# Chunk work moved between the steps of the first block, one fused attention and two-layer kernel

## The chip, the cores and the metric

The kernel runs on one core of one Trainium2 chip. The metric is device microseconds of one execution of the whole program, from launch to end, the median over runs. The core has a matrix engine (PE, with PEld for its weight loads), a vector engine (DVE), a scalar engine (ACT), a general engine (POOL), and a sync engine (SP) whose queue issues all DMAs here. Each engine takes its own instructions in the order in which they were written.

## The reference

```
for t in range(S):                                    # B=4, H=8, S=768, D=48
    state = alpha[:, :, t, :, None] * state + einsum('bhd,bhe->bhde', k[:, :, t], v[:, :, t])
    y[:, :, t] = einsum('bhd,bhde->bhe', q[:, :, t], state)
x = y.transpose(0, 2, 1, 3).reshape(B * S, H * D)     # 3072 tokens x 384
h = x @ w_in ;  x = (max(h, 0) + m_alpha * min(h, 0)) @ w_out          # 384 -> 2048 -> 384
h = x @ w_in2;  out = where(h >= 1, h, where(h <= -1, 0, (h + 1)**2 / 4)) @ w_out2
```

A linear attention with a decay per channel and token feeds two dense layers. The four weight matrices arrive as 64-bit floats and are turned into 32-bit floats on the chip.

## The kernel before

**Attention.** The tokens are cut into 24 chunks of 128, six in each batch element. For a chunk c the kernel transposes the decays (`fetch(c, 2)`, line 210 on PE, then `clamp` on DVE, line 202), the keys (`fetch(c, 1)`) and the queries (`fetch(c, 0)`). Two scans over the decays follow on DVE: `at_scan(c, "R")` (line 257) and `at_scan(c, "F")` (lines 263 and 264). `K2` is the keys times R, `Q2` the queries times F (line 274). `at_kt` transposes K2 back (`kt`, line 280 on PE) and ACT copies it to SBUF (`KT`, line 282). `at_gain` (line 337), `at_states` and `at_decay` carry the state from chunk to chunk, `at_within` makes the scores inside a chunk (lines 305 and 319, then `A`, line 324), and `at_out` (lines 372 and 305) the outputs, which ACT and DVE split into a high and a low word in `xs` (lines 394 to 401); six small DMAs (line 408) bring the shared rows to their place. The transposes of decays, keys, queries and K2 of the chunks 4 to 9 all use one PSUM tile, tag `at`, with a single buffer: each must be read out before the next is written. The chunks 10 and later are transposed on DVE instead.

**Layers.** A step is one block of 512 tokens by one of 16 slices (`fc`) of the hidden dimension. `do_h(s)` makes nine matmuls `hp` (line 512), ACT then scales them (`g`, line 526), DVE takes the maximum (line 530), ACT rounds it to `gh` (line 531), DVE makes the remainder `gl` (line 533). `do_out(s - 1)` follows on PE with nine matmuls from the step before (line 553). The products keep a high and a low word of both operands, hence nine. Block 0 is the tokens of the chunks 0 to 3, so those four run first, in the opening, a loop over `c` of its own; the steps s = 0 to 15 are block 0.

**Weights.** In block 0 each step also prepares later weights. `w1_load(fc + 5)` issues seven DMAs into one of three buffers; `w1_words` makes two ACT passes over the 32-bit words of the 64-bit floats (part 0 is line 440, part 1 line 442), in place; `w1_join(fc + 2)` puts them together in two DVE passes (lines 448 and 451), which frees the buffer; `w1_split` makes the high word on ACT (`wh`, line 490) and the low one on POOL (`wl`, line 496), which the matmuls two steps later need.

**What sets the order.** The kernel writes the order out by hand. Four tables say what chunk work goes where: `pres[s]` ahead of step s, `acts[s]` inside `emit_act` between `gh` and `gl`, `mids[s]` after `do_h(s)` and its weights, `ends[s]` after `do_out(s - 1)`. A chunk c of 4 to 7 starts at step s = 2 + 3(c - 4) and takes n = 3 steps, later ones n = 4. Where `acts` has an entry, both join passes of the step stand ahead of `hp`'s maximum; otherwise one does, and the other stands between `gh` and `gl`. `fetch(c, 0)` also issues the loads of chunk c + 2 on SP, behind the six small DMAs of `at_out`.

Of the kernel before, what the change touches and what calls it, by code (L numbers as in the profile page):

```python
# [22 lines left out]
def kernel(  # L23
# [593 lines left out]
    def put(where, s, *fs):  # L617
        where.setdefault(s, []).extend(fs)
# [4 lines left out]

    put(mids, 0, lambda: fetch(NC0, 2))
    put(ends, 0, lambda: at_scan(NC0, "R"), lambda: fetch(NC0, 1), lambda: at_mul(NC0, "K2", nc.vector))
    put(mids, 1, lambda: at_scan(NC0, "F"))
    put(ends, 1, lambda: at_kt(NC0), lambda: at_decay(NC0))
    put(acts, 2, lambda: fetch(NC0 + 1, 2))
    for c in range(NC0, NCH + 1):
# [11 lines left out]
        if c + 1 < NCH:  # L641

            put(pres if s + 1 < NFC else ends, s + 1, lambda c=c: at_scan(c + 1, "R"))
            if c + 1 < NPE:
                put(ends, s + (n - 2 if direct(c + 1, 1) else 1), lambda c=c: fetch(c + 1, 1))
            put(ends, s + n - 2, lambda c=c: at_mul(c + 1, "K2", nc.vector))
            put(ends, s + n - 1, lambda c=c: at_kt(c + 1), lambda c=c: at_decay(c + 1))
            put(pres if s + n - 1 < NFC else ends, s + n - 1, lambda c=c: at_scan(c + 1, "F"))
        if c + 2 < NPE:
            put(acts, s + 2, lambda c=c: fetch(c + 2, 2))  # L650
        if c == NPE - 2:
# [9 lines left out]
    with tc.manual_schedule():  # L661
# [8 lines left out]
        def w1_words(i, part=None):  # L670
            if 0 <= i < NFC:
                conv_words(0, i, part)
# [119 lines left out]
        for c in range(NC0):  # L792
# [6 lines left out]
            if c < NC0 - 1:  # L799
                at_kt(c + 1)  # L800
            if c + 2 < NC0:
                at_scan(c + 2, "R")
                at_scan(c + 2, "F")
# [15 lines left out]
            if i >= 0:  # L819
                w1_split(i)  # L820
        load_chunk(NC0 + 1, nc.sync)
        mps = ps_h.tile([P, NFC], F32, tag="h", name="mps", padded_shape=[P, 512])
        nc.tensor.transpose(out=mps, in_=ma, identity=ident[0:NFC, 0:NFC])
# [3 lines left out]
        for s in range(len(steps) + SK):  # L827
            if s < len(steps):
                j, fc = steps[s]
                if j == 0:  # L830
                    full = s in acts
                    run_slots(pres, s)
                    w1_join(fc + 2, None if full else 0)
                do_h(s, (lambda: w1_words(fc + 3, 0),
                         lambda: run_slots(acts, s) if full else w1_join(fc + 2, 1)) if j == 0 else None)
# [7 lines left out]
            if s < NFC:  # L843
                w1_words(fc + 3, 1)
            if s < len(steps):
# [197 lines left out]
```

## Time and profile before

| | us |
|---|---|
| median of 3 runs (lowest to highest) | 945.85 (945.71 to 948.45) |
| the profiled execution, its own time | 945.43 |
| its span, first to last instruction | 943.6 |
| PE busy | 905.5 |
| DVE busy | 482.2 |
| ACT busy | 406.7 |
| POOL busy | 361.4 |

The time of the profiled execution lies 1.8 us above its span: that is launch and end. In the rows below block 0 is cut where the `hp` of a step starts: step 0 at 40.94 us, step 2 at 55.49, step 5 at 75.97, step 8 at 97.51, step 11 at 120.38, step 14 at 139.84. PE is busy for nearly all of the span; its idle time stands almost wholly in the first 155 us, which are the opening and block 0. The mean granted TensorE clock is 0.987 of 2.4 GHz; the stretches at half of it stand in the same 155 us.

### The profile page before, as it was taken

The page shows a single profiled execution, that of the slowest core. Times are in us where ns is not written, and L with a number is a line of the kernel's source. Part 1 is how long each engine was busy: PE and PEld are TensorE (multiplying, and loading weights), DVE is VectorE, ACT ScalarE, POOL GpSimd, SP SyncE. Part 2 cuts the span into 40 slices and gives each one's busy share as a digit, 9 for nine tenths or more (in the row PEclk, how much of TensorE's full clock was granted, in tenths as well). Part 3 has the DMA queues.
Part 4 walks back from the last instruction along what each step waited for, and adds up shares of the span by engine and source line. Part 5 has one row for each costly group of instructions (what it writes and reads, how often), then busy time and mean ns, then how long its engine had stood idle before and what let it go on. Part 6 is the DMA issues. An engine that isn't in the chain of part 4 may idle for free.

```text
span 943.6 us, 17329 instructions
## 1 busy us (share of the span) xinstructions
PE 905.5 (96%) x6955; PEld 770.2 (82%) x6955; DVE 482.2 (51%) x692; ACT 406.7 (43%) x654; POOL 361.4 (38%) x294
## 2 busy tenths in 40 slices
PE   7787899999999999999999999999999999999996
PEld 5676677788888788788788899999999999999995
DVE  7598764766765666665322234435334334344333
ACT  2555554443444434444355533345554333333332
POOL 4233222643544344443267732332332332333231
PEclk9899999999999999999999999999999999999999
DMA  9785735554654545442143210212220200200001
GB/s 165 173 164 125 167 87 160 137 141 124 190 140 124 145 113 155 130 128 65 42 161 107 76 60 1 77 47 62 84 67 1 67 1 1 68 1 1 34 1 38
DMA packets 119897, 85.58 MB, mean 91 GB/s; under 512 B 64752, under 2 KB 105472, under 8 KB 119808
## 3 DMA queue, kind: packets, MB, share of 16 engines
q1 hardware_dynamic: 119808, 84.39, 34.5%
q8 instruction: 56, 0.92, 0.4%
q14 instruction: 33, 0.27, 0.1%
HBM read 66.66 MB, written 15.73 MB: 87 GB/s over the span
## 4 chain that ended last, share of the span: by engine, by line
PE 87%; DVE 4%; DMA 3%; SPq 2%; issue 2%; ACT 2%; DVEq 0%; ACTq 0%
PE hp L512 40%; PE y_oo L553 12%; PE y_yy L564 7%; PE y_oo L564 7%; PE y_o L553 6%; PE y_o L564 3%; PE y_at L564 3%; DMA nat<-in_alpha_dram 2%; PE w L372 1%; SPq L408 1%; PE w L305 1%; PE kt L280 1%; PE w L337 1%; PE tr L210 1%; PE w L319 1%
## 5 line engine op out<-in xcount | busy, mean ns | idle before, releaser
L544 POOL TENSOR_TENSOR gl<-g,gh 128x512 fp32r<-128x512 f32 x175 | 233.4, 1333 | 454.3 <-ACT gh L543 444.2
L512 PE MATMUL hp<-xs,wh 128*128 128x512 f32 x1152 | 367.8, 401 | 3.8 <-issue 3.2
L512 PEld LDWEIGHTS hp<-xs,wh 128*128 128x128 f32 x1152 | 212.1, 190 | 44.0 <-issue 4.9
L512 PE MATMUL hp<-xs,wl 128*128 128x512 f32 x576 | 227.9, 396 | 0.0
L543 ACT CAST gh<-g 128x512 fp32r<-128x512 f32 x177 | 109.4, 618 | 211.5 <-DVE g L542 143.9
L540 DVE SCALAR_TENSOR_TENSOR g<-g 128x512 f32<-128x512 f32 (+1 forms) x97 | 67.7, 697 | 207.7 <-ACT g L524 206.3
L512 PEld LDWEIGHTS hp<-xs,wl 128*128 128x128 f32 x576 | 109.3, 190 | 24.1
L526 ACT ACTIVATE g<-hp,malpha 128x512 f32<-128x512 f32 x96 | 66.2, 689 | 139.2 <-PE hp L512 139.1
L538 DVE TENSOR_TENSOR g<-hp,g 128x512 f32<-128x512 f32 x80 | 55.2, 690 | 102.7 <-ACT g L526 102.2
L524 ACT ACTIVATE g<-hp,half 128x512 f32<-128x512 f32 (+1 forms) x97 | 66.5, 686 | 94.0 <-PE hp L512 94.0
L542 DVE TENSOR_TENSOR g<-hp,g 128x512 f32<-128x512 f32 (+1 forms) x97 | 66.5, 686 | 3.4
L496 POOL TENSOR_TENSOR wl<-wf,wh 128x768 fp32r<-128x768 f32 x16 | 30.5, 1904 | 79.5 <-ACT wh L490 59.5
L553 PE MATMUL y_oo<-gh,wh 128*128 128x512 f32 x192 | 60.5, 397 | 0.0
L553 PE MATMUL y_oo<-gl,wh 128*128 128x512 f32 x192 | 60.1, 394 | 0.4 <-POOL gl L544 0.4
L553 PE MATMUL y_oo<-gh,wl 128*128 128x512 f32 x192 | 60.0, 394 | 0.0
L243 DVE STREAM_TRANSPOSE T<-nat 128x512 f32<-128x512 f32 x42 | 43.4, 1086 | 0.0
L553 PEld LDWEIGHTS y_oo<-gl,wh 128*128 128x128 f32 x192 | 36.3, 189 | 8.6 <-POOL gl L544 0.8
L553 PEld LDWEIGHTS y_oo<-gh,wl 128*128 128x128 f32 x192 | 36.4, 189 | 7.9
L553 PEld LDWEIGHTS y_oo<-gh,wh 128*128 128x128 f32 x192 | 36.1, 190 | 7.4
L399 DVE TENSOR_TENSOR xs<-w,xs 128x384 fp32r<-128x384 f32 x24 | 13.4, 557 | 50.4 <-ACT x L398 45.5
L210 PE MATMUL tr<-ident,nat 128*128 128x128 f32 x120 | 23.0, 328 | 16.7 <-DMA nat<-in_alpha_dram 11.4
L553 PE MATMUL y_o<-gl,wh 128*128 128x512 f32 x96 | 38.1, 396 | 0.0
(127 smaller groups left out, 1397.2 us busy)
## 6 DMA issues: line engine op xcount, KB each, us to landing
wst<-in_moe_w_out_dram SPq DMA_DIRECT2D x32, 384.0 KB, 4.6
wst<-in_moe_w_in_dram SPq DMA_DIRECT2D x16, 384.0 KB, 4.2
w_d<-wf SPq DMA_DIRECT2D x16, 384.0 KB, 2.7
w<-w_d SPq DMA_DIRECT2D x16, 384.0 KB, 3.1
x_d<-ev SPq DMA_DIRECT2D x18, 256.0 KB, 2.3
x2s<-x_d SPq DMA_DIRECT2D x18, 256.0 KB, 3.6
out_dram<-ev SPq DMA_DIRECT2D x24, 192.0 KB, 2.0
al<-in_alpha_dram SPq DMA_DIRECT2D x12, 384.0 KB, 3.3
```

Of the source, the lines that this page charges most:

```text
L210: nc.tensor.transpose(out=ps[:, p, :], in_=nat_of(c, i)[:, 2 * p:2 * p + 2, :].rearrange("t h d -> t (h d)"), identity=ident)
L243: nc.vector.transpose(out=tin(c, i).rearrange("f n (j g) -> f n g j", g=4), in_=natq[:, n].rearrange("j n (g f) -> j n g f", g=4)[:, :, :, ...
L512: nc.tensor.matmul(out=hp, lhsT=w[:, p, :], rhs=xs[:, x, p, :], start=(i == 0), stop=(i == 3 * ND - 1))
L524: nc.scalar.activation(y, x, AF.Relu, bias=half, scale=0.5)
L526: nc.scalar.activation(y, x, AF.Copy, scale=malpha[:, fc:fc + 1])
L538: nc.vector.tensor_max(out=y, in0=x, in1=y)
L540: nc.vector.scalar_tensor_tensor(out=y, in0=y, scalar=1.0, in1=y, op0=ALU.min, op1=ALU.mult)
L542: nc.vector.tensor_max(out=y, in0=x, in1=y)
L543: nc.scalar.copy(out=hi, in_=y)
L544: (nc.gpsimd if parts == 1 else nc.vector).tensor_sub(out=lo, in0=y, in1=hi.bitcast(F32))
L553: nc.tensor.matmul(out=ops[d], lhsT=w[:, d * P:(d + 1) * P], rhs=g, start=first, stop=last)
L564: nc.tensor.matmul(out=ops[t], lhsT=g[:, t * P:(t + 1) * P], rhs=w, start=first, stop=last)
```

## The change

Four things are written in another place. No arithmetic, tile or DMA is added or dropped.

- The decays of a chunk (`fetch(c, 2)`, with the clamp) are transposed in `acts` of the first step of chunk c - 1; before, they were in the last step of chunk c - 2. `acts` thus has entries at the steps 2, 5, 8, 11 and 14 and not at 2, 4, 7, 10 and 13.
- `at_kt`, the transpose of K2, goes from `ends` to `mids` of the same step (while that step is below 16), that is ahead of `do_out`.
- The two word passes are half a step earlier: part 0 of the weights `fc + 4` at the end of a step, part 1 of `fc + 3` inside `emit_act`. Before, it was part 0 of `fc + 3` inside and part 1 of `fc + 3` at the end.
- The decays, R, keys, K2 and F of chunk 4 are made in the opening, in and behind its last pass, and its `at_kt` in step 0; before, they stood in the steps 0 and 1.

```diff
-    put(mids, 0, lambda: fetch(NC0, 2))
-    put(ends, 0, lambda: at_scan(NC0, "R"), lambda: fetch(NC0, 1), lambda: at_mul(NC0, "K2", nc.vector))
-    put(mids, 1, lambda: at_scan(NC0, "F"))
-    put(ends, 1, lambda: at_kt(NC0), lambda: at_decay(NC0))
-    put(acts, 2, lambda: fetch(NC0 + 1, 2))
+    put(mids, 0, lambda: at_kt(NC0))
+    put(ends, 0, lambda: at_decay(NC0))
...
-            put(ends, s + n - 1, lambda c=c: at_kt(c + 1), lambda c=c: at_decay(c + 1))
+            put(mids if s + n - 1 < NFC else ends, s + n - 1, lambda c=c: at_kt(c + 1))
+            put(ends, s + n - 1, lambda c=c: at_decay(c + 1))
...
-        if c + 2 < NPE:
-            put(acts, s + 2, lambda c=c: fetch(c + 2, 2))
+        if c + 1 < NPE:
+            put(acts, s, lambda c=c: fetch(c + 1, 2))
...
             if c < NC0 - 1:
                 at_kt(c + 1)
+            else:
+                fetch(NC0, 2)
+                at_scan(NC0, "R")
...
         load_chunk(NC0 + 1, nc.sync)
+        fetch(NC0, 1)
+        at_mul(NC0, "K2", nc.vector)
+        at_scan(NC0, "F")
...
-                do_h(s, (lambda: w1_words(fc + 3, 0),
+                do_h(s, (lambda: w1_words(fc + 3, 1 if s else None),
...
-                w1_words(fc + 3, 1)
+                w1_words(fc + 4, 0)
```

The first place is DVE, from the end of the opening to the first `gl`. `T` is the clamped decay of chunk 4, `R`, `K` and `F` are its scans and keys, `wf` the joined weights, `A` the scores of chunk 3. Before:

```order
L324 TENSOR_TENSOR A<-w,mask 128x512
L448 SCALAR_TENSOR_TENSOR wf<-wst 128x768
L399 TENSOR_TENSOR xs<-w,xs 128x3x128
L451 SCALAR_TENSOR_TENSOR wf<-wst,wf 128x768
L448 SCALAR_TENSOR_TENSOR wf<-wst 128x768
L530 TENSOR_TENSOR hp<-hp,g 128x512
L451 SCALAR_TENSOR_TENSOR wf<-wst,wf 128x768
L533 TENSOR_TENSOR gl<-hp,gh 128x512
L202 TENSOR_SCALAR T_104<-tr 128x4x128
L257 SCALAR_TENSOR_TENSOR R<-T_104,zrev 128x516
L274 TENSOR_TENSOR K_738<-tr,R 128x512
```

Now:

```order
L324 TENSOR_TENSOR A<-w,mask 128x512
L202 TENSOR_SCALAR T_104<-tr 128x4x128
L257 SCALAR_TENSOR_TENSOR R<-T_104,zrev 128x516
L448 SCALAR_TENSOR_TENSOR wf<-wst 128x768
L399 TENSOR_TENSOR xs<-w,xs 128x3x128
L451 SCALAR_TENSOR_TENSOR wf<-wst,wf 128x768
L274 TENSOR_TENSOR K_702<-tr,R 128x512
L263 RECIPROCAL zfw<-R 128x4
L264 SCALAR_TENSOR_TENSOR F<-T_104,zfw 128x516
L448 SCALAR_TENSOR_TENSOR wf<-wst 128x768
L530 TENSOR_TENSOR hp<-hp,g 128x512
```

The clamp and R now stand ahead of the last xs of the opening, K2 and F ahead of the first maximum.

The second place is ACT in the steps 4 and 5, with one chunk's `KT` copy. Before:

```order
L526 ACTIVATE g<-hp,malpha 128x512
L440 ACTIVATE wst<-wst 128x768
L531 CAST gh<-hp 128x512
L490 CAST wh_991<-wf 128x768
L282 COPY KT<-kt 128x512
L442 ACTIVATE wst<-wst,mhalf 128x768
```

Now:

```order
L440 ACTIVATE wst<-wst 128x768
L526 ACTIVATE g<-hp,malpha 128x512
L442 ACTIVATE wst<-wst,mhalf 128x768
L531 CAST gh<-hp 128x512
L490 CAST wh_986<-wf 128x768
L282 COPY KT<-kt 128x512
```

The word pass L440 now stands ahead of the activation of `hp`, and L442 between that and `gh`; the `KT` copy still stands behind `gh` and `wh`.

The third place is PE from the end of `hp` of step 4 to the beginning of step 5. Before:

```order
L512 MATMUL hp<-xs,wl_834 128x512
L210 MATMUL tr<-ident,nat 128x128 x4
L553 MATMUL y_oo<-gh,wh_770 128x512 x2
...
L553 MATMUL y_o_778<-gl,wh_770 128x512
L280 MATMUL kt<-ident,K_950 128x128 x4
L512 MATMUL hp<-xs,wh_906 128x512 x2
```

Now:

```order
L512 MATMUL hp<-xs,wl_835 128x512
L280 MATMUL kt<-ident,K_951 128x128 x4
L553 MATMUL y_oo<-gh,wh_782 128x512 x2
...
L512 MATMUL hp<-xs,wl_909 128x512
L210 MATMUL tr<-ident,nat 128x128 x4
L553 MATMUL y_oo<-gh,wh_833 128x512 x2
```

`kt` takes the place of the decays' transpose behind `hp`, and the decays' transpose stands a step later, behind the next `hp`.

## Rows read from the trace of the kernel before

**Rows 1.** The page's busy time of each engine, share of the span, instructions.

```profile
PE 905.5 (96%) x6955; PEld 770.2 (82%) x6955; DVE 482.2 (51%) x692; ACT 406.7 (43%) x654; POOL 361.4 (38%) x294
```

**Rows 2.** Stretches: us, busy PE, PEld, DVE, ACT, POOL (instructions), clock, DMA share, GB/s.

```profile
40.94:55.49 14.55, 11.51 (x40) 9.00 (x40) 10.87 (x13) 8.26 (x12) 3.64 (x2) 0.73 0.87 190
55.49:75.97 20.48, 16.69 (x158) 13.22 (x156) 19.86 (x26) 12.28 (x17) 7.49 (x4) 1.00 0.68 150
75.97:97.51 21.54, 18.42 (x185) 14.68 (x184) 16.46 (x23) 12.82 (x19) 7.27 (x5) 0.92 0.58 127
97.51:120.38 22.87, 19.72 (x194) 15.85 (x193) 16.26 (x23) 12.43 (x18) 7.28 (x5) 0.86 0.74 173
120.38:139.84 19.46, 17.20 (x192) 13.54 (x191) 16.09 (x23) 11.66 (x17) 3.68 (x2) 0.99 0.37 75
```

**Rows 3.** Timeline of PE: start, length, line, tiles, idle before and releaser.

```profile
48.94 1.12 PE L210 MATMUL tr<-ident,nat 128*128 128x128 f32 x4 [3.04 <-DVE T L202]
62.41 0.66 PE L210 MATMUL tr<-ident,nat 128*128 128x128 f32 x4 [1.49 <-DVE T L202]
75.55 0.66 PE L280 MATMUL kt<-ident,K 128*128 128x128 f32 x4 [2.31 <-DVE T L202]
94.61 0.63 PE L210 MATMUL tr<-ident,nat 128*128 128x128 f32 x4 [3.12 <-DMA nat<-in_alpha_dram]
114.60 1.09 PE L210 MATMUL tr<-ident,nat 128*128 128x128 f32 x4 [3.15 <-DMA nat<-in_alpha_dram]
```

**Rows 4.** The chain that ended last: start, length, what.

```profile
50.05 3.19 PE hp L512 x9
76.21 3.66 PE hp L512 x9
97.75 2.08 PE hp L512 x9
```

**Rows 5.** Timeline of DVE and PE at the end of the opening.

```profile
36.62 0.69 PE L372 MATMUL w<-A,v 64*64 64x64 f32 x32 [1.77 <-DVE A L324]
40.92 0.56 DVE L399 TENSOR_TENSOR xs<-w,xs 128x384 fp32r<-128x384 f32 x1 [3.49 <-ACT xs L394]
45.11 0.79 PE L210 MATMUL tr<-ident,nat 128*128 128x128 f32 x4
46.13 0.70 DVE L530 TENSOR_TENSOR hp<-hp,g 128x512 f32<-128x512 f32 x1 [2.54 <-ACT g L526]
```

**Rows 6.** Timeline of DVE: the two scans, at their longest and shortest.

```profile
48.92 2.68 DVE L257 TENSOR_TENSOR_SCAN R<-T,zrev 128x516 f32<-128x516 f32 x1
85.49 1.22 DVE L257 TENSOR_TENSOR_SCAN R<-T,zrev 128x516 f32<-128x516 f32 x1
70.43 2.03 DVE L264 TENSOR_TENSOR_SCAN F<-T,zfw 128x516 f32<-128x516 f32 x1
```

**Rows 7.** Timeline of DVE, ACT and PE in step 4.

```profile
69.63 0.68 DVE L274 TENSOR_TENSOR K<-tr,R 128x512 f32<-128x512 f32 x1
70.57 0.60 PE L210 MATMUL tr<-ident,nat 128*128 128x128 f32 x4
74.21 0.69 DVE L530 TENSOR_TENSOR hp<-hp,g 128x512 f32<-128x512 f32 x1
75.42 0.84 ACT L490 CAST wh<-wf 128x768 fp32r<-128x768 f32 x1
76.25 0.59 ACT L282 COPY KT<-kt 128x512 f32<-128x512 f32 x1
```

**Rows 8.** Timeline of SP's queue and ACT around a chunk's outputs.

```profile
87.11 3.94 SPq L408 DMA_DIRECT2D xs<-x  x6
91.10 0.58 SPq L177 DMA_DIRECT2D nat<-in_alpha_dram  x1
99.93 0.69 ACT L526 ACTIVATE g<-hp,malpha 128x512 f32<-128x512 f32 x1 [0.67 <-PE hp L512]
101.09 0.93 ACT L440 ACTIVATE wst<-wst 128x768 f32<-128x768 f32 x1 [0.47 <-DMA wst<-in_moe_w_out_dram]
```

## The prediction, made before the changed kernel ran

> **What bounds the kernel now.** I read the page first: PE is busy for 905.5 us of a span of 943.6 [rows 1], so only PE's 38 us of idle time, and matmuls that run at half clock, can be won. Next the busy time in stretches, to see where the idle time stands: between the `hp` of step 0 and that of step 14 there are 98.9 us, of which PE is busy 83.5 [rows 2]; the reader is to take busy from length in each row: 3.04, 3.79, 3.12, 3.15 and 2.26 us idle. The timeline of PE then names what ended each of the long waits [rows 3]: two of them DMA of a chunk's decays (3.12 and 3.15), the others the clamp L202, which frees the one PSUM buffer that the next transpose needs (3.04, 1.49, 2.31). Last the chain, for the price of the clock: nine `hp` matmuls take 2.08 us at 2.4 GHz, but 3.19 and 3.66 behind two of the gaps [rows 4], where a stretch at 1.2 GHz follows. DVE is the next bound: it is busy 16.1 to 16.5 us of the 19.5 to 22.9 of three steps [rows 2].
>
> **The sum, stretch by stretch.** All terms are changes against the profiled execution, 945.43 us.
>
> *Opening, up to hp of step 0: +1.0.* The clamp (0.68) and R go ahead of the last xs of the opening; R takes 1.22 to 2.68 [rows 6], long where POOL's wl runs beside it, as it does here. DVE waited 3.49 us just there [rows 5], so both fit. K2 (0.68), the reciprocal (0.17) and F (1.23 to 2.08) meet an idle time of 2.54 ahead of the first maximum [rows 5]: they fit or overrun by 0.4. PE gets two transposes of 0.79 to 1.12 us at half clock [rows 3, 5]; the first stands where PE waited 1.77 for A [rows 5] and costs nothing unless its decays land late, the second is in front of `hp`. Bounds 0 and +1.9, the two together; I take +1.0, the second at its longer price.
>
> *Steps 0 and 1: -5.3.* The wait of 3.04 goes, with the two transposes 0.79 and 1.12 [rows 3, 5]: -4.9. Without that gap the hp of step 1 runs at full clock: 3.19 - 2.08 = -1.1 [rows 4]. Back come 0.7: in step 0 both word passes stand ahead of gh on ACT, and the second, a pass of about 0.9 [rows 8], pushes gh, for which PE then waits. If the clock falls all the same, this term is -4.2.
>
> *Steps 2 to 4: -2.2.* The wait of 2.31 was the clamp of a transpose in step 4, which is now in step 5: it goes, and so does that transpose's own 0.4 on PE's path (of the 0.60 that it is busy [rows 7], as its end overlaps what follows). The 1.49 of step 2 stays: order and work are the same there. I add 0.5 for a new wait: `kt` moves ahead of `do_out`, so K2 must be ready some 2.1 us earlier. In step 4 K2 ended at 69.63 + 0.68 = 70.31, and `hp` at 70.57 [rows 7], so 0.26 is left; as PE closes up by more, some of it is lost. Bounds 0 and 1.0.
>
> *Steps 5 to 7: -3.3.* The decays now have a step more to land: they were issued at 91.10 [rows 8] and awaited until 94.61 [rows 3], 3.5 us, and are used a full step (some 6 us) later: -3.1. The half clock behind the 2.31 goes: 3.66 - 2.08 = -1.6 [rows 4]. New is a wait on the KT copy. The transpose of the decays writes the PSUM buffer that `kt` filled the step before, and ACT empties it only behind gh and wh, and wh waits for DVE's second join. With the rows of step 4: K2 starts at 69.63, then F, a join, the maximum and a join end at 74.21 + 0.69 = 74.9 whatever their order [rows 7]; wh begins there, and the copy ends 0.83 + 0.59 behind the start of wh (75.42 to 76.84) [rows 7], so at 76.3. PE, from hp's end at 70.57, has kt (0.4 to 0.6, as that transpose), `do_out` and hp (nine matmuls each, 2.08 to 2.2 [rows 4]) and comes to 75.1 to 75.6, I take 75.4. So +0.9; bounds 0 (F 0.8 shorter, as the scans can be [rows 6]) and 1.3. With 0.5 for K2 as above: -3.1 - 1.6 + 0.9 + 0.5.
>
> *Steps 8 to 10: -4.1.* The wait of 3.15 goes. Behind it, from 114.60 to the hp at 120.38 PE took 5.78 us at half clock; the same work behind the earlier gap, 94.61 to 97.51, took 2.90 [rows 2, 3]: -2.9. Again +0.9 and +0.5. And +0.5 for the word pass L440, which now stands ahead of the activation L526. Its weights are issued behind six small DMAs and three loads of a chunk. Before, they landed at 101.09, 25.1 us after the hp of step 5 began at 75.97. Half clock (-1.6) is in that. So is SP's queue, which a weight load held until the small DMAs began at 87.11; that load's join is now written ahead of the maximum, which frees the queue sooner by 0 to 4.8 us (no row tells; I take the middle, 2.4). With 0.9 for KT it is 22.0. The hp of step 8 ends 18.1 + 2.1 = 20.2 us after that of step 5 began (18.1: 21.5 less the 3.3 above). So L526 is late by 1.8 and the pass, 2.7. The clamp behind it has about that slack or more, as `do_out` (2.1), the chunk's outputs (0.69 for L372 alone [rows 5]) and its gain stand on PE ahead of the transpose that needs it; but DVE, 16.3 of 18.1 us busy, has 1.8 to spare, and loses some 0.9. I take half of it; bounds 0 and 3.
>
> ACT did wait for such a weight, 0.47 us at 101.09 [rows 8], and nothing on PE followed. The Trainium skill (TensorE: Matmul & The Clock Gate, Architectural detail) says that ScalarE and VectorE take their queues strictly first in, first out, which speaks against the move: whatever stands ahead of L526 holds it. By that rule the full 2.7 or more would go through in each chunk; by the row the cost was nil, since the pass stood behind the activation. It is rival 2 below.
>
> *Steps 11 to 13: -0.4.* Of 2.26 idle all goes [rows 2]; back come 0.9, 0.5 and 0.5 as before. *Steps 14 and 15: +1.3.* The last decays' transpose (0.4) moves in here, with its wait for KT (0.9).
>
> 1.0 - 5.3 - 2.2 - 3.3 - 4.1 - 0.4 + 1.3 = -13.0. Past step 15 PE is bound by its own matmuls, and nothing is moved, so the gain is kept. On the profiled execution: 932.4; on the median of 945.85, which is 0.4 higher: 932.9.
>
> **Rivals.**
>
> 1. *All hides (928).* KT and K2 cost nothing, as F runs at 1.23 rather than 2.03: 4 x 0.9 and 3 x 0.5 less, about -18. For it: the scans do run at 1.22 where POOL is idle [rows 6]. Against: wl runs once a step.
>
> 2. *ACT's queue holds the activations (939).* The word pass waits 2.7 or more behind the chunk's DMAs, and DVE, with no slack, hands it on to PE: +3 in each of two chunks. For it: the rows above and the order. Against: half of the chunks' weights are loaded with the queue free, and the last steps have no loads.
>
> 3. *DVE becomes the pace (937).* Busy 16.3 of three steps, with waits between its ops it needs 20 us for three, not 18.1. The three stretches then give -1.5, -2.9 and +0.5 instead of -7.8: 1.0 - 5.3 - 2.2 - 3.9 + 1.3 = -9.1.
>
> 4. *The load chain makes it slower (951).* If the weights come so late that L526 waits 4.8 us in each of the four chunks' first steps (2.7, and 2.1 more if the queue comes free no sooner) and PE gets all of it: 4 x 4.8 = 19.2 against 14.0 of gain without the two word-pass terms: +5.2. It decides from 14.0 / 4 = 3.5 us a chunk. Against it: the loads are not written later than before, and in just these steps PE has the chunk's outputs to do as well.
>
> 5. *No change (945.6).* From step 2 on the DMA gaps turn into DVE gaps of the same size, and the half clock stays: 1.0 - 5.3 for the opening and the steps 0 and 1, three waits for KT (2.7) and the +1.3 of the end: -0.3. For it: DVE is busy 19.86 of 20.48 in the steps 2 to 4 [rows 2]. Against: 16.3 of 21.5 and less behind them.
>
> **How the numbers follow.** The forecast of 932.9 has a chance of 0.52, its own range is 929 to 937 (KT 0 to 1.3 four times, K2 0 to 1.0 three times, the opening 0 to 1.9, seldom all at one end). Rival 1 has 0.13, rival 2 0.13, rival 3 0.12, rival 4 0.05, rival 5 0.05. Half clock that stays in one place would add 1.1 to 2.9. Eight times in ten I expect 926.5 to 941.5: it takes in the rivals 1 to 3, and leaves out 4 and 5. What a measurement of this kernel can tell from no change is about 0.3%, 943.0 to 948.7: rivals 1 to 3 and the forecast lie below it, so faster has 0.89 (0.90 less 0.01 that may reach into it); same 0.06, slower 0.05.
>
> **What would show it.** In the changed profile, PE's waits on DMA of `nat` are gone or under 1 us; a wait of a decays' transpose on ACT's KT copy of about 0.9 us stands in the steps 5, 8, 11 and 14; no transpose waits over 1 us ahead of step 2; the granted clock is 1.0 from step 1 on; three steps take 18 to 19 us; L526 starts late behind L440 in the steps 8 and 11, and PE does not follow. It is wrong if PE waits longer than 1.5 us for gh, gl or Q in these steps, if the clock falls again, or if the hp of step 14, which by the sum starts at 139.84 - 14.3 = 125.5, starts behind 130.

## The result and the profile after

The changed kernel took 936.63 us (median of 8), the kernel before, taken beside it, 947.9 (median of 8): a ratio of 0.9897, with a 95% interval of 0.9869 to 0.9925. Faster was right, and the time lies in the range, with 0.4 us to spare; the gain is smaller than forecast. The profiled executions say by how much: 945.43 before, 936.41 after, a gain of 9.0 where the sum had 13.0. One execution of each kernel (5042 us of the changed one, 1009 of the one before) is left out of the ratio.

The page of the changed kernel, its first row (busy time, share of the span, instructions), answers to [rows 1]:

```profile
PE 903.9 (97%) x6955; PEld 767.8 (82%) x6955; DVE 487.9 (52%) x692; ACT 405.4 (43%) x654; POOL 362.9 (39%) x294
```

PE's busy time fell by 1.6 us, the span by 9.0, but the 1.6 is the sum of two opposite terms. From the first `hp` of step 0 to that of step 16, PE's idle time fell by 5.9 (16.05 to 10.18) and its busy time by 5.5 (95.57 to 90.07), of which 1.9 are the two transposes that went to the opening and the rest is mostly half clock. In the opening the busy time rose by 3.6 (30.23 to 33.80), as the transposes came in and PE is at half clock up to 45.7 us. (Of the 38 us that PE was idle before, 26.8 stand ahead of step 16, not nearly all.) The stretches of the changed kernel, cut at the same steps as [rows 2] (steps 0–1, 2–4, 5–7, 8–10, 11–13, 14–15; us, busy PE, PEld, DVE, ACT, POOL, clock, DMA share, GB/s):

```profile
43.54:52.38 8.84, 8.32 (x32) 6.18 (x32) 8.27 (x10) 6.95 (x11) 3.46 (x2) 0.88 0.70 144
52.38:71.80 19.42, 16.30 (x151) 12.82 (x150) 17.52 (x21) 12.82 (x18) 7.50 (x5) 1.00 0.84 184
71.80:89.63 17.83, 16.94 (x183) 13.44 (x182) 17.11 (x23) 12.31 (x18) 7.05 (x4) 1.00 0.55 143
89.63:111.76 22.13, 18.52 (x192) 14.68 (x190) 18.72 (x26) 12.39 (x19) 5.86 (x3) 0.92 0.85 174
111.76:129.25 17.49, 17.12 (x191) 13.44 (x190) 16.52 (x22) 10.51 (x16) 7.05 (x4) 1.00 0.57 125
129.25:143.79 14.54, 12.86 (x181) 10.08 (x180) 9.40 (x16) 5.59 (x10) 2.31 (x2) 1.00 0.13 24
```

The reader takes each length from that of [rows 2], with one correction. The cuts there at 120.38 and 139.84 lie inside an `hp`; its first matmul, which is the cut everywhere else, starts at 120.03 and 139.60 (timeline of PE, before):

```profile
120.03 0.96 PE L512 MATMUL hp<-xs,wh 128*128 128x512 f32 x2
...
139.60 0.70 PE L512 MATMUL hp<-xs,wh 128*128 128x512 f32 x2
```

So steps 8 to 10 took 22.52 before, steps 11 to 13 took 19.57, and steps 14 and 15 took 152.56 − 139.60 = 12.96:

| stretch | forecast | measured |
|---|---|---|
| opening, to the first hp (40.94 to 43.54) | +1.0 | +2.6 |
| steps 0–1 | −5.3 | −5.7 |
| steps 2–4 | −2.2 | −1.1 |
| steps 5–7 | −3.3 | −3.7 |
| steps 8–10 | −4.1 | −0.4 |
| steps 11–13 | −0.4 | −2.1 |
| steps 14–15 | +1.3 | +1.6 |
| behind step 15 | 0 | −0.2 |

One row is far off: steps 8 to 10 were to give 4.1 and gave 0.4. The timeline of PE in the changed kernel has the waits that answer to [rows 3] (steps 2, 5, 8, 8, 11–13, 14):

```profile
61.14 0.66 PE L210 MATMUL tr<-ident,nat 128*128 128x128 f32 x4 [2.52 <-DVE T L202]
...
74.92 0.66 PE L210 MATMUL tr<-ident,nat 128*128 128x128 f32 x4 [0.89 <-ACT KT L282]
...
92.93 0.66 PE L210 MATMUL tr<-ident,nat 128*128 128x128 f32 x4 [1.07 <-ACT KT L282]
...
99.51 0.66 PE L210 MATMUL tr<-ident,nat 128*128 128x128 f32 x4 [2.54 <-DVE T L202]
99.93 0.84 PE L512 MATMUL hp<-xs,wh 128*128 128x512 f32 x2
...
103.55 0.74 PE L553 MATMUL y_oo<-gh,wh 128*128 128x512 f32 x2
...
126.68 0.66 PE L280 MATMUL kt<-ident,K 128*128 128x128 f32 x4 [0.32 <-DVE K L274]
...
132.48 0.66 PE L210 MATMUL tr<-ident,nat 128*128 128x128 f32 x4 [1.00 <-ACT KT L282]
```

The waits for DMA of `nat` are gone, all of them. The waits for the KT copy are there at the forecast size (0.89, 1.07, 1.00). And a clamp, L202, holds PE for 2.54 us in step 8, where the sum had 0.5. The hp behind it takes 103.55 − 99.93 = 3.62 us in place of 2.08: a stretch at 1.2 GHz, as this row of the busy time by stretches of the changed kernel has it:

```profile
100.40:103.80 3.40, 3.40 (x10) 2.65 (x9) 2.97 (x6) 1.30 (x3) 1.80 (x1) 0.50 0.90 203
```

What makes the clamp late is seen on ACT and DVE (timeline of the changed kernel, steps 2 and 8; the row of PE is the last matmul of step 8's `hp`, which L526 needs):

```profile
58.28 0.91 ACT L440 ACTIVATE wst<-wst 128x768 f32<-128x768 f32 x1 [2.57 <-DMA wst<-in_moe_w_in_dram]
59.09 0.67 ACT L526 ACTIVATE g<-hp,malpha 128x512 f32<-128x512 f32 x1
...
91.46 0.40 PE L512 MATMUL hp<-xs,wl 128*128 128x512 f32 x1
...
96.68 0.88 ACT L440 ACTIVATE wst<-wst 128x768 f32<-128x768 f32 x1 [3.80 <-DMA wst<-in_moe_w_in_dram]
97.46 0.68 ACT L526 ACTIVATE g<-hp,malpha 128x512 f32<-128x512 f32 x1
98.17 0.70 DVE L530 TENSOR_TENSOR hp<-hp,g 128x512 f32<-128x512 f32 x1 [2.66 <-ACT g L526]
98.78 0.68 DVE L202 TENSOR_SCALAR T<-tr 128x512 f32<-128x512 f32 x1
```

The word pass L440 waits for its weights, the activation L526 stands behind it, the maximum L530 waits for that, and the clamp is written behind the maximum. In step 8 `hp` ends at 91.86 and L526 starts at 97.46, 5.6 us later. This is the mechanism of rival 2, in steps 2 and 8 rather than 8 and 11. The weights of step 8 are issued late by SP's queue (timeline of SP, same kernel):

```profile
82.52 3.95 SPq L408 DMA_DIRECT2D xs<-x  x6
86.52 0.58 SPq L177 DMA_DIRECT2D nat<-in_alpha_dram  x1
...
88.65 1.15 SPq L430 DMA_DIRECT2D wst<-in_moe_w_in_dram  x2
...
91.72 1.71 SPq L434 DMA_DIRECT2D wst<-in_moe_w_out_dram  x1
```

From 82.5 to 93.4 SP does nothing but issue: six small DMAs (3.95), three loads of a chunk, then the seven DMAs of the weights that L440 waits for, of which the last is issued at 91.72 to 93.43 (1.71 us, where the same line takes 0.42 elsewhere; why is not seen). They have landed at 96.68, 3.25 us behind that.

### The profile page after: what moved, and what is told of

Read it like the earlier page. It is cut to its first block, busy times and chain, and to the rows that moved or that the text cites. A ratio compares the mean times of both kernels' runs of the same rounds, so it can differ in the third digit from the quotient of the medians.

```text
span 934.6 us, 17309 instructions
## 1 busy us (share of the span) xinstructions
PE 903.9 (97%) x6955; PEld 767.8 (82%) x6955; DVE 487.9 (52%) x692; ACT 405.4 (43%) x654; POOL 362.9 (39%) x294
## 4 chain that ended last, share of the span: by engine, by line
PE 81%; DMA 7%; DVE 5%; SPq 3%; ACT 2%; issue 1%; DVEq 0%; ACTq 0%
PE hp L512 37%; PE y_oo L553 11%; PE y_yy L564 7%; PE y_oo L564 7%; PE y_o L553 5%; PE y_o L564 3%; PE y_at L564 3%; DMA wst<-in_moe_w_in_dram 2%; DMA wst<-in_moe_w_out_dram 2%; SPq L408 1%; PE w L372 1%; PE w L305 1%; DVE wf L451 1%; DMA xs<-x 1%; PE w L337 1%
## 5 line engine op out<-in xcount | busy, mean ns | idle before, releaser
L526 ACT ACTIVATE g<-hp,malpha 128x512 f32<-128x512 f32 x96 | 66.0, 688 | 130.1 <-PE hp L512 130.1
L553 PE MATMUL y_o<-gh,wh 128*128 128x512 f32 x96 | 37.6, 391 | 0.0
```

The lines of the kernel that those rows point to most:

```text
L526: nc.scalar.activation(y, x, AF.Copy, scale=malpha[:, fc:fc + 1])
L553: nc.tensor.matmul(out=ops[d], lhsT=w[:, d * P:(d + 1) * P], rhs=g, start=first, stop=last)
```

## The experiments

The theory: what rival 2 describes cost steps 8 to 10 their gain, by way of the word passes, and SP's issuing is behind it. The rivals: that the KT copy or the keys' place cost it; that the DMA engines themselves are the limit; that whatever is taken away in one place turns up in the next. All variants are edits of the changed kernel unless it says otherwise. "Block 0" is the time from the first hp of step 0 to that of step 16 in the profiled execution; it holds all that the change moves but the opening.

| kernel | block 0, us | median, us (runs) | ratio to before, 95% interval |
|---|---|---|---|
| before | 111.62 | 946.9 to 948.8 (five groups) | 1 |
| changed | 100.25 | 936.63 (8) | 0.9897 (0.9869–0.9925) |
| changed, again | 100.03 | 940.33 (10) | 0.9914 (0.988–0.9949) |
| words back | 101.32 | 937.49 (10) | 0.9918 (0.9877–0.9958) |
| KT early | 100.47 | 936.27 (10) | 0.9883 (0.9834–0.9932) |
| keys back | 99.95 | 934.22 (4) | 0.9884 (0.9805–0.9963) |
| xs late | 99.66 | 937.47 (4) | 0.9898 (0.9818–0.9978) |
| opening only | 104.59 | 943.28 (10) | 0.996 (0.9925–0.9996) |
| decays back | 118.25 | 953.63 (10) | 1.0061 (1.003–1.0092) |
| one load | 97.31 | 932.77 (4) | 0.9817 (0.9756–0.9879) |
| xs late, KT early | 99.87 | 935.32 (4) | 0.9843 (0.9779–0.9906) |
| opening and decays | 100.37 | 938.43 (4) | 0.9882 (0.9834–0.993) |
| xs on GpSimd | 99.15 | 986.7 (5) | 1.0398 (1.0357–1.0438) |
| less on SP | 96.93 | 934.63 (4) | 0.9883 (0.9843–0.9924) |

Half clock takes a hand in some of these. In words back, KT early, opening and decays, and xs on GpSimd the `hp` of step 3 runs at half clock: from it to the `hp` of step 4 they take 7.0 to 7.2 us, all the others 5.6. That is 1.4 to 1.6 us of their block 0. It stands behind waits of 3.15, 2.93, 3.14 and 1.76 us, while keys back has a wait of 2.72 in the same place and no half clock; with one profile each it is not shown whether it belongs to the edit or to the execution.

**The changed kernel again.** No edit.

> The changed kernel itself, beside the two others of this job. Both theories: stretch from step 0 to step 16 within 0.7 us of 100.3 and the same waits in steps 2, 5, 8 and 14 (2.5, 0.9, 1.1 with 2.5, 1.0). If the waits in steps 2 and 8 differ by more than 1 us, they hang on when the loads land from one execution to the next, and differences of that size between the other variants tell nothing.

Block 0 took 100.03, the waits were 2.20, 0.88, 1.07 with 2.27, and 0.99: the pattern repeats within 0.4 us. Differences in block 0 can be read down to about 1 us where the half clock stands in the same places, and to about 1.6 where it does not. The whole time can't be read so finely. Behind step 96 the same code runs at one of three paces; the stretch from the hp of step 96 to that of step 191 in the changed kernel, first of its first and then of its second profile:

```profile
525.50:919.96 394.46, 394.18 (x1994) 357.97 (x1993) 159.59 (x217) 159.82 (x269) 126.98 (x97) 1.00 0.11 35
```

```profile
525.95:926.64 400.69, 400.41 (x1994) 362.14 (x1992) 159.51 (x217) 160.33 (x269) 126.50 (x97) 1.00 0.11 34
```

It is 394.5, 398.2 or 400.7 us in all fourteen profiles, and nothing that the variants edit runs there. Medians that differ by a few us are therefore no verdict on an edit, and the variants are compared by block 0.

**Words back.** The two word passes of a step where they were before.

```diff
-                do_h(s, (lambda: w1_words(fc + 3, 1 if s else None),
+                do_h(s, (lambda: w1_words(fc + 3, 0),
...
-                w1_words(fc + 4, 0)
+                w1_words(fc + 3, 1)
```

> The word passes stand where they stood before the change, all else is as changed. Theory (ACT's queue): in the changed kernel L440 waits 2.57 us in step 2 and 3.80 us in step 8 for its weights and holds the activation behind it, and PE's waits of 2.52 and 2.54 us for the clamp, with the half clock after the second (1.3), are its price. With the pass behind the activation step 8's wait falls under 0.5 and step 2's to about 1.5, as before the change; no half clock; the span falls by about 4.8 us, to 930. Rival (the early pass is what keeps DVE's joins from waiting): the joins wait 1 to 1.5 us a step for L442, PE waits for gh or the clamp in other steps, and the span stays at 934 or rises.

In step 8 the clamp's wait fell from 2.54 to 0.46, the half clock behind it went, and steps 8 to 10 took 19.83 in place of 22.13: the mechanism is right. But block 0 grew by 1.1, as the rival had it: steps 2 to 4 took 1.9 more and steps 11 to 13 took 1.6 more. In step 2 the wait is 3.15, and the clock falls behind it (timeline of ACT, DVE and PE, words back):

```profile
55.76 0.98 ACT L442 ACTIVATE wst<-wst,mhalf 128x768 uint32<-128x768 uint32 x1
...
56.77 1.88 DVE L448 SCALAR_TENSOR_TENSOR wf<-wst 128x768 uint32<-128x768 uint32 x1 [1.19 <-DMA wst<-in_moe_w_out_dram]
...
60.90 0.94 PE L210 MATMUL tr<-ident,nat 128*128 128x128 f32 x4 [3.15 <-DVE T L202]
```

The profile names a load as what the join L448 waited for, but these weights had landed: the first pass, L440, had read them at 52.54. What L448 needs last is the second pass, L442, which stands behind `gh` and `wh` again and ends at 56.74. The join starts 0.03 us later, with maximum and clamp behind it. In the first steps of the later chunks (5, 8 and 11) the join waits 1.7 us for L442 each time, and in the kernel before the join of step 2 (57.83) starts as L442 ends as well. Later there are waits for K (1.14), KT (1.00) and clamps (0.66 and 0.65) that the changed kernel hasn't. So the place of the passes is a trade: early, L440 with its late weights holds the activation; late, L442 holds the join.

**KT early.** The KT copy ahead of gh and wh on ACT.

```diff
-    put(mids, 0, lambda: at_kt(NC0))
+    kts = {}
+    put(kts, 0, lambda: at_kt(NC0))
...
-            put(mids if s + n - 1 < NFC else ends, s + n - 1, lambda c=c: at_kt(c + 1))
+            put(kts if s + n - 1 < NFC else ends, s + n - 1, lambda c=c: at_kt(c + 1))
...
-                do_h(s, (lambda: w1_words(fc + 3, 1 if s else None),
+                do_h(s, (lambda: (w1_words(fc + 3, 1 if s else None), run_slots(kts, s)),
```

> The K2 transpose keeps its place on PE, but its copy on ACT stands ahead of gh and wh instead of behind them. Theory: the waits of 0.89, 1.07 and 1.00 us for the copy (steps 5, 8, 14) vanish; steps 5 and 14 give 1.9 us; the 1.07 of step 8 only lengthens the wait for the clamp there, which the weights' DMA sets. Span about 932.7. Rival (the copy is late because K2 is late, not for its place in ACT's queue): ACT now waits at the copy with gh behind it, PE waits for gh, and nothing is won.

The three waits for KT are gone, and steps 5 to 7 and 14 to 15 are shorter by 1.2 and 1.3, a little more than expected. Block 0 is the same (100.47) because steps 2 to 4 are longer by 1.9: step 2's wait is 2.93 there, and the half clock of step 3 follows. In step 8 PE now waits in one piece for what it waited for in two (1.07 and 2.54); ACT and PE, KT early:

```profile
96.05 0.90 ACT L440 ACTIVATE wst<-wst 128x768 f32<-128x768 f32 x1 [4.66 <-DMA wst<-in_moe_w_in_dram]
...
98.90 1.12 PE L210 MATMUL tr<-ident,nat 128*128 128x128 f32 x4 [4.07 <-DVE T L202]
```

So KT's 1.07 in step 8 was free: L440 gets its weights 7.3 us behind the start of step 8's `hp` here and 7.1 in the changed kernel, and PE waits for them once or in two pieces.

**Keys back.** The transpose of the keys at the end of the step, as before.

```diff
-            put(mids if s + n - 1 < NFC else ends, s + n - 1, lambda c=c: at_kt(c + 1))
+            put(ends, s + n - 1, lambda c=c: at_kt(c + 1))
```

> The K2 transpose of the later chunks stands at the end of its step again, the other three parts as changed. Theory: the copy then comes right behind it in ACT's queue, a whole hp (2.1 us) ahead of the decays' transpose, so the three waits of about 1 us vanish and no wait comes at the transpose itself, since the clamp that it waited for (2.31 us before the change) is no longer in its step: 1.9 us less, span about 932.7, so this part of the change costs time. Rival (the key transpose in mid-step pays): waits of over 1 us come back at the K2 transpose, span 936 or more.

The waits for KT did not go; they are 0.89, 1.17 and two of 1.5. I had not seen that the copy's place on ACT stays the same, behind wh (timeline of ACT, keys back):

```profile
91.34 0.83 ACT L490 CAST wh<-wf 128x768 fp32r<-128x768 f32 x1 [0.27 <-DVE wf L451]
92.08 0.58 ACT L282 COPY KT<-kt 128x512 f32<-128x512 f32 x1
```

Block 0 is 99.95: the keys' new place is worth nothing by itself.

**xs late.** The six xs DMAs a step later, behind that step's weights on SP.

```diff
-            nc.sync.dma_start(out=xs[64 * a + D:64 * a + 64, :, p, o:o + C].bitcast(F32),
-                              in_=x3[r:r + 16].bitcast(F32))
+            late.append(lambda p=p, a=a, r=r: nc.sync.dma_start(
+                out=xs[64 * a + D:64 * a + 64, :, p, o:o + C].bitcast(F32), in_=x3[r:r + 16].bitcast(F32)))
...
                     w1_load(fc + 5)
+                    while late:
+                        late.pop(0)()
```

> The six small DMAs of a chunk's outputs are issued a step later, behind the weights' seven, all else as changed. Theory (SP's queue sets when the weights land): the weights of step 8's pass are issued 4 us sooner, L440's wait of 3.80 us falls to under 0.5, PE's 2.54 and the half clock go, span about 930.8; step 2 stays as it is, since no small DMAs are issued there. Rival (bandwidth or latency sets the landing): the weights land at most 1 us sooner, and the span stays at 934.

The clamp's wait in step 8 is gone altogether, so the six DMAs ahead of the weights in SP's queue did cause it. Only 0.6 us of block 0 came of it, as the next weights, now behind the xs, are late a step further on (timelines of ACT, DVE and PE, xs late, step 9 to 10):

```profile
101.23 0.90 ACT L440 ACTIVATE wst<-wst 128x768 f32<-128x768 f32 x1 [4.85 <-DMA wst<-in_moe_w_out_dram]
...
102.74 0.70 DVE L530 TENSOR_TENSOR hp<-hp,g 128x512 f32<-128x512 f32 x1 [2.32 <-ACT g L526]
...
105.41 0.68 DVE L274 TENSOR_TENSOR K<-tr,R 128x512 f32<-128x512 f32 x1
...
106.15 0.66 PE L280 MATMUL kt<-ident,K 128*128 128x128 f32 x4 [2.57 <-DVE K L274]
```

The same chain, L440, L526, L530, now holds K instead of a clamp.

**xs late and KT early** together.

> The changed kernel with the xs DMAs a step later and the KT copy ahead of gh and wh together. Theory, that the waits are separate: the KT waits (0.9, 1.1, 1.0) and the clamp's wait in step 8 are all gone, stretch from step 0 to step 16 about 97 us (changed 100.3, xs late alone 99.7, KT early alone 100.5). Rival, that the weights' arrival and VectorE's queue pace these steps: what is taken away stands elsewhere as a wait for K or a clamp, 99 us or more.

The rival was right. Block 0 is 99.87, with waits of 1.35 and 1.81 for the clamp and these for K (timeline of PE):

```profile
107.22 0.66 PE L280 MATMUL kt<-ident,K 128*128 128x128 f32 x4 [1.61 <-DVE K L274]
...
127.57 0.66 PE L280 MATMUL kt<-ident,K 128*128 128x128 f32 x4 [2.39 <-DVE K L274]
```

**Opening only.** The kernel before, with the decays, clamp and scans of chunk 4 in the opening, and nothing else.

```diff
-    put(mids, 0, lambda: fetch(NC0, 2))
-    put(ends, 0, lambda: at_scan(NC0, "R"), lambda: fetch(NC0, 1), lambda: at_mul(NC0, "K2", nc.vector))
-    put(mids, 1, lambda: at_scan(NC0, "F"))
...
+            else:
+                fetch(NC0, 2)
+                at_scan(NC0, "R")
...
+        fetch(NC0, 1)
+        at_mul(NC0, "K2", nc.vector)
+        at_scan(NC0, "F")
```

> The kernel before with only the opening of the change in it (decays, clamp and both scans of chunk 4 in the opening; decays of later chunks, keys and word passes stay where they were). Theory, that the parts add up by stretch: steps 0 and 1 lose their waits of 3.04 and 1.49 us and the half clock (14.55 us down to about 9), the opening grows by about 1, and the waits for nat alpha of 3.12 and 3.15 us in steps 8 and 11 stay; from the first hp of step 0 to that of step 16 about 106 us (before 111.6, changed 100.3). Rival, that the loads set the pace from step 2 on: the time won in steps 0 and 1 is lost again by step 8, and the stretch takes 109 us or more.

Block 0 is 104.59, 7.0 less than before; steps 0 and 1 take 9.19. Of what they gained (5.4), steps 2 to 4 lose 2.0 again, with a new wait of 1.74 for the KT copy in step 2. The waits of steps 8 and 11 are where they were, and not shorter (timeline of PE, opening only):

```profile
92.38 0.63 PE L210 MATMUL tr<-ident,nat 128*128 128x128 f32 x4 [3.27 <-DMA nat<-in_alpha_dram]
...
112.91 0.63 PE L210 MATMUL tr<-ident,nat 128*128 128x128 f32 x4 [3.69 <-DMA nat<-in_alpha_dram]
```

**Decays back.** The changed kernel with the decays transposed in a chunk's third step, two chunks ahead, as before.

```diff
+    put(acts, 2, lambda: fetch(NC0 + 1, 2))
...
-        if c + 1 < NPE:
-            put(acts, s, lambda c=c: fetch(c + 1, 2))
+        if c + 2 < NPE:
+            put(acts, s + 2, lambda c=c: fetch(c + 2, 2))
```

> The changed kernel with the transposes of the decays back in a chunk's third step, two chunks ahead. Theory: they are the part that took away the waits for nat alpha, so one to two waits of about 3 us with that releaser come back in steps 8 and 11, and the stretch from step 0 to step 16 is 104 us or more (changed 100.3). Rival, that the load chain had taken over by then: the waits for nat alpha come back and the clamp's waits in the same steps go, stretch within 1.5 us of 100.3.

It is slower than the kernel before: block 0 takes 118.25, 13.7 more than with the opening alone. A wait for `nat` alpha came back in step 8, as expected (2.89; one of 3.83 in step 11 the profile puts down to a join), and a worse one with it, which I had not foreseen (timelines of PE and DVE, decays back, step 4):

```profile
68.19 0.60 PE L210 MATMUL tr<-ident,nat 128*128 128x128 f32 x4
...
72.43 0.68 DVE L202 TENSOR_SCALAR T<-tr 128x512 f32<-128x512 f32 x1
...
73.16 1.11 PE L280 MATMUL kt<-ident,K 128*128 128x128 f32 x4 [4.38 <-DVE T L202]
```

With the keys in mid-step, `kt` stands right behind the decays' transpose of the same step. Both need the one PSUM buffer, which the clamp empties behind F, both passes of a join and the maximum on DVE; `do_out`, which lay between them before, now waits as well, and half clock follows. The parts of the change are not independent: the keys can be in mid-step only because the decays are in another step. The 13.7 is the price of keys and word passes together; the waits of `kt` (4.38 in step 4, 3.70 in step 13, 0.79 twice) put most of it on the keys, but no run has them alone.

**Opening and decays.** The changed kernel with words back and keys back, both edits shown above.

> The changed kernel with the keys back at the end of a step and the word passes back where they were: the opening and the decays alone are changed. Theory, that these two parts carry the whole gain, and that keys and word passes only move waits about: from the first hp of step 0 to that of step 16 between 99.5 and 101.5 us (before 111.6, opening alone 104.6, changed 100.3), and the median within 2 us of the changed kernel's in this job. Rival, that keys in mid-step are worth something once the decays are out of their way: 102.5 us or more.

Block 0 is 100.37: these two parts carry the whole gain, 7.0 and 4.2. Keys and word passes together bring neither gain nor loss that one profile can show (1.6 of the 100.37 is the half clock in step 3). In step 8 the clamp's wait is 0.46, as with words back alone, and KT's waits are larger (1.30, 1.55, 1.54).

**One load.** The six DMAs of a step's first-layer input weights as one of the same bytes and row length. It reads the second layer's array, so its output is another and only its time is of use.

```diff
-            for a in range(2):
-                for b in range(2):
-                    n = slice(0, NP // 2) if a == b else slice(NP // 2, ND)
-                    eng.dma_start(out=ti[64 * a:64 * a + D, n], in_=wv[b][:, n])
-                eng.dma_start(out=ti[64 * a + D:64 * a + 64], in_=wg[a])
+            eng.dma_start(out=ti, in_=w_in2[:, f].rearrange("(p i) f -> i p f", i=P))
```

> The changed kernel with the six DMAs of a step's first-layer input weights put into one of the same bytes and row length (their words are taken from the second layer's array, so the output is another). SP issues two DMAs a step in place of seven, some 0.8 us in place of 3. Theory, that SP's issue queue (3.94 us for the six xs DMAs, then 2.1 for nat, then the weights) makes L440 wait in step 8: the clamp's wait of 2.54 us there goes, the half clock behind it too, and the stretch from step 0 to step 16 is 97.5 us or less (changed 100.3). In step 2, where the DMA engines were busy at 0.96, the wait of 2.52 us stays above 1.5. Rival, that the bytes bound both places: both waits stay above 1.5 us, stretch above 99.

Block 0 fell to 97.31. The clamp's wait went from 2.54 to 0.89 in step 8, without half clock, and from 2.52 to 1.09 in step 2, where I had expected it to stay above 1.5 because the DMA engines were busy at 0.96. So it is not the bytes alone that set the weights' arrival, in either place, but the issuing or the split into many DMAs; the last variant, which keeps the DMAs as they are, speaks for the issuing. SP's weights (timeline, one load; its lines are 3 or 4 lower):

```profile
86.29 1.28 SPq L427 DMA_DIRECT2D wst<-in_moe_w_in_dram  x1
87.62 0.48 SPq L430 DMA_DIRECT2D wst<-in_moe_w_out_dram  x1
```

**xs on GpSimd.** The six xs DMAs issued by GpSimd.

```diff
-            nc.sync.dma_start(out=xs[64 * a + D:64 * a + 64, :, p, o:o + C].bitcast(F32),
+            nc.gpsimd.dma_start(out=xs[64 * a + D:64 * a + 64, :, p, o:o + C].bitcast(F32),
```

> The changed kernel with the six xs DMAs of a chunk issued by GpSimd in place of SP, so that 3.94 us of issuing no longer stand ahead of nat and of the weights on SP. Theory (issue queue): in step 8 L440's wait of 3.80 us for its weights falls below 1.5 us, the clamp's wait behind it goes from 2.54 to below 1, and step 0 to step 16 takes 98.5 us or less. Rival, that what counts is the sum of what is asked of the DMA engines, or that GpSimd's own issue is slower than SP's and holds its subtractions (L496) back: waits of 1 us or more for wl or xs appear, stretch 100 us or more.

Neither forecast was met in block 0: it is 99.15, L440's wait in step 8 is 2.67 (from 3.80) and the clamp's 1.44 (from 2.54), with no wait for wl above 0.5. The whole kernel is slower, 986.7. The rival's loss came where I hadn't looked. Behind block 0 GpSimd does Q's product, which then waits behind the six DMAs (timeline of PE, then of GpSimd):

```profile
164.36 0.52 PE L305 MATMUL w<-Q,bd 48*64 48x64 f32 x16 [2.13 <-POOL Q L274]
```

```profile
159.97 3.04 POOL L408 DMA_DIRECT2D xs<-x  x6 [1.94 <-issue]
163.03 1.28 POOL L274 TENSOR_TENSOR Q<-T,F 128x512 f32<-128x512 f32 x1
```

There are fifteen such waits, of 2.1 to 2.4 (32.7 in all), and the stretch from step 16 to step 96 takes 429.6 in place of 381.7, at a granted clock of 0.96 in place of 1.00.

**Less on SP.** Drawn from the two before: xs on GpSimd for the chunks of block 0 only, and the two gate DMAs of each step's weights too.

```diff
-                eng.dma_start(out=ti[64 * a + D:64 * a + 64], in_=wg[a])
+                if own.get("gate"):
+                    gate.append(lambda a=a, ti=ti: nc.gpsimd.dma_start(out=ti[64 * a + D:64 * a + 64], in_=wg[a]))
+                else:
+                    eng.dma_start(out=ti[64 * a + D:64 * a + 64], in_=wg[a])
...
-            nc.sync.dma_start(out=xs[64 * a + D:64 * a + 64, :, p, o:o + C].bitcast(F32),
+            (nc.gpsimd if c < 2 * NC0 else nc.sync).dma_start(out=xs[64 * a + D:64 * a + 64, :, p, o:o + C].bitcast(F32),
...
+                    own["gate"] = True
                     w1_load(fc + 5)
                     w1_split(fc + 2)
+                    while gate:
+                        gate.pop(0)()
```

> The changed kernel with two kinds of DMA of the first block issued by GpSimd in place of SP: the six xs of chunks 4 to 7, and the two L431 of each step's weights (issued behind that step's L496). SP keeps five DMAs a step for the weights in place of seven, some 2.1 us in place of 3. Theory (SP's issue queue is the limit where the weights come late): L440's waits in steps 2 and 8 fall below those of the changed kernel (2.57 and 3.80 us), no wait for wl appears, and step 0 to step 16 takes 98.5 us or less (changed 100.3 and again 100.0, xs on GpSimd alone 99.2). Rival, that GpSimd has to wait for a free wst buffer before it can issue and holds back the next L496: waits for wl of 1 us or more, 100 us or more.

Block 0 takes 96.93, 3.1 to 3.3 less than in the changed kernel's two profiles; L440's waits fell to 1.98 in step 2 and 1.36 in step 8, as the theory had it. This row is block 0 of it, by busy time (columns as above):

```profile
42.92:139.85 96.93, 89.26 (x924) 70.12 (x924) 87.54 (x114) 60.30 (x90) 55.65 (x65) 0.98 0.72 154
```

The clamp's wait in step 8 is gone, with the half clock, the one in step 2 is 1.55, and none for wl is above 0.5. The median is 934.63. Whether the whole is faster than the changed kernel the ratios don't tell, as the intervals overlap; its profile ran at the pace of 398.2 behind step 96, that of the changed kernel at 394.5, and still its span is 2.0 shorter (932.6 and 934.6).

## Why the prediction was right or wrong

**Right: steps 0 and 1.** 5.3 was forecast, 5.7 measured, and the opening alone gave 5.4 there (14.55 to 9.19). The wait of 3.04, the two transposes and the half clock in step 1 went as the rows said.

**Right: the loads of the decays.** None of the DMA waits is left, and with the decays back the one of step 8 was back.

**Right: the KT copy.** 0.9 was forecast for steps 5, 8, 11 and 14; 0.89, 1.07 and 1.00 stand in 5, 8 and 14, none in 11. KT early shows the cost to be real in steps 5 and 14 (1.2 and 1.3 less without it) and nothing in step 8, where the weights are what PE waits for.

**Partly: the opening.** +2.6 against +1.0. The products of chunk 2 at L305 start at 29.45 in the changed trace and at 27.95 in the one before, ahead of anything that was moved: 1.5 of it lies between the executions, and 1.1 is left for the moved work. The thirteen profiles with this opening come to their first hp at 41.82 to 44.47, so one of them can't size this term.

**Wrong: when the weights land in steps 8 to 10, the mis-sized term.** The word pass L440 was given 0.5, with bounds 0 and 3. PE waited 2.54, and the clock fell for one hp more, 3.62 in place of 2.08: 4.1 where 0.5 was written. That excess of 3.6, with 0.2 more for KT and less the 0.5 for K that was not paid, is what is missing, once the half clock's 2.9 is put right: with the hp at 120.03 it is 2.5, and the sum for these steps −3.8, not −4.1. The chain was right: L526 was held, as the Trainium skill (TensorE: Matmul & The Clock Gate, Architectural detail) has it, and the trace agrees: L440 waits 3.80 and L526 starts as it ends.

The step that failed is the landing. Counted from the start of step 5's hp, the weights were to land at 22.0 and L526 to be 2.7 late; they landed at 24.9 (25.1 before), and L526 was 5.6 late. The slack of the clamp was there, 5.6 − 2.54 = 3.1, enough for a delay of 2.7, but not for 5.6. The landing did not move because SP's queue did not come free sooner. For that I took 1.6 for the half clock and 2.4, "the middle", for the join that is written earlier. The join that frees the buffer, step 5 (timeline of DVE, before and changed):

```profile
81.28 0.95 DVE L451 SCALAR_TENSOR_TENSOR wf<-wst,wf 128x768 uint32<-128x768 uint32 x1
```

```profile
75.01 2.49 DVE L451 SCALAR_TENSOR_TENSOR wf<-wst,wf 128x768 uint32<-128x768 uint32 x1
77.57 0.78 SPq L430 DMA_DIRECT2D wst<-in_moe_w_in_dram  x2
```

It ends 6.3 us behind the start of that hp before and 5.7 in the changed kernel: 0.6 sooner where 4.0 was taken. It started earlier, but took 2.49 beside wl, and DVE had been busy without a pause since F at 69.16; the load is issued as the join ends. That the rest of the sum for these steps held is shown by less on SP: there the weights land at 22.3, and steps 8 to 10 take 18.66, where the sum had 22.52 − 3.8 = 18.7. Rival 2 had the mechanism and priced it at 3 a chunk, in two chunks; one chunk paid 4.1, and step 2 a part.

**Wrong by half: steps 2 to 4.** I had the 1.49 of step 2 stay, as order and work are the same. The order is not: the change moves the word passes there too. Before, the join behind L442 ended that wait; in the changed kernel the join is early (L448 at 55.36), and L440, which waits 2.57 for its weights, holds the activation. The wait grew to 2.52, a wait of 0.60 for wl came, and the 0.5 for K was not paid: 1.1 in all. Part of it is that PE came to step 2 3.1 us earlier, and the wait ended only 1.27 earlier.

**Better than forecast: steps 11 to 13**, by 1.7. L440 waited 1.30 there and PE did not follow, no KT wait appeared, and K cost 0.3. PE had already lost that time in step 8: in words back, one load, xs on GpSimd and less on SP, where step 8's wait is smaller or gone, a KT wait of 1.0 stands in step 11.

**Of the signs named:** the DMA waits, the KT waits (but in step 11) and the missing waits ahead of step 2 held. "Three steps take 18 to 19" held in none of the four stretches: two are longer (19.42, 22.13), two shorter (17.83, 17.49). That PE does not follow L526 failed in step 8. The clock fell once more, at 100.4, which the prediction itself had named as a sign of being wrong, and the hp of step 14 came at 129.25, between the forecast 125.5 and the 130 named as the limit.

**Luck in the number.** The sum was 4.0 too large on the profiled executions, which ran at the same pace behind step 96. That the median still lies in the range hangs on the executions taken: the same kernel again has a median of 940.33, outside the range of 929 to 937, and the three paces alone are up to 6.2 apart. (In rival 4 the 14.0 should be 14.2, as the two word-pass terms are 0.7 and 0.5; nothing hangs on it.)

**What the gain hangs on** is shown: opening and decays, 11.3 of block 0's 11.4. That step 8's weights come late for SP's issuing is shown by xs late, which reorders it, and by three kernels that take issues away (97.31, 99.15, 96.93). Left open is what is still behind step 2's wait when SP issues less (1.09 and 1.55), whether a shorter queue would also make KT early pay, and what brings the half clock in step 3; none was tried.

## What to carry to other kernels

A wait that ends with a DMA's landing has a date of its own: what is won ahead of it is lost in it (KT early, step 8). The date is that of the issue, and the issue waits for a buffer: follow that back to the instruction that frees it, here a join on DVE, before taking a gain on it. Moving the instruction that waits chooses which queue it blocks, and its old place may have kept another wait away. Parts of a reordering share buffers: test them singly and in what they leave out, since here keys and word passes cost 13.7 us without the decays and nothing with them. Where several edits move less than the executions differ by, compare the stretch that they touch, not the whole time.

## What the runs showed of the hardware

With a granted clock of 1.00 and PE idle for 0.28 us in all, the same 95 steps took 394.46, 398.20 or 400.69 us, the changed kernel itself the first and the last; the mean hp matmul (wh) took 390 ns in the one and 397 in the other. What sets the pace isn't seen in the trace.

Issuing is work that a queue can be short of: the six xs DMAs of 16 KB took SP 3.95 us (GpSimd 3.04), and six DMAs made one were worth 2.9 us of block 0 (100.25 to 97.31). The Trainium skill (DMA: Bandwidth & Descriptors, Issuing engines are not separate DMA queues) has it that issuing from several engines saves only the sequencers' time, which is usually small beside the transfer; here taking a part of it off SP was worth 3.1 to 3.3 us of block 0. The page Perfetto Trace Analysis (DMA Optimizations) of the Trainium skill has it that balancing over the issuing engines may help where the issuing engine is what is busy; less on SP agrees (96.93), and xs on GpSimd shows the other side, as a product that PE needs stood behind the DMAs in GpSimd's queue.

The join L451 takes 0.95 us, and 2.48 where GpSimd's wl ran beside it (93.03 in the changed trace, wl from 92.53 to 94.69); it ends 0.8 us behind wl.
